# Leaving 110 groups of constant products out of a planned two-layer attention kernel, with a new order for every engine

## The chip, the core and the metric

The kernel runs on one core of a Trainium2 chip. The metric is device time in microseconds (us) of one execution: the lower, the better. TensorE is called PE, VectorE DVE, ScalarE ACT, GpSimd POOL, and SyncE, which issues most of the DMAs, SP. L944 is line 944 of the kernel before.

## The reference, cut to what matters

Four attention layers in a row, A, B, A, B, each added to its input (2048 positions, 512 features, 32 heads of 16):

```
def _A_ref(x, wqkv, wo):          # window of 8 positions, 2 apart
    q, k, v = split(x @ wqkv)
    logits = einsum("bhsd,bhswd->bhsw", q, k[pos - 2*w]) * scale
    o = einsum("bhsw,bhswd->bhsd", softmax(masked logits), v[pos - 2*w])
    return o @ wo
def _B_ref(x, wqkv, wo):          # causal, the last 256 positions
    scores = masked(einsum("bhqd,bhkd->bhqk", q, k) * scale)
    return einsum("bhqk,bhkd->bhqd", softmax(scores), v) @ wo
x = x + _A_ref(_layernorm(x), A_wqkv, A_wo)
x = x + _B_ref(_layernorm(x), B_wqkv, B_wo)
x = x + _A_ref(_layernorm(x), A_wqkv, A_wo)
x = x + _B_ref(_layernorm(x), B_wqkv, B_wo)
```

## The kernel before, in words

The 2048 positions are cut into 8 chunks of 256. For each of the two A, B pairs of layers and each chunk, `layer_a` and then `layer_b` add their work to a plan, so that there are 16 units A0, B0, A1, B1 to A15, B15. Ahead of them `prep` (scopes pA and pB) loads the weights and splits each into two fp16 parts.

Every piece of work is a task on one engine. A layer normalises (`norm`, L875: statistics on DVE at L888, the power at L897 on POOL, the scaled copy `xn` at L915 on ACT, four transposes on PE at L919, the halves `xh` on ACT and `xl` on DVE), projects (`proj_t`, L944 to L946, and `proj_n`, L964 to L967, on PE, three fp16 products for each fp32 one), attends and then projects out (`finish`, L978: `oh` on ACT, `ol` on POOL or DVE, `proj_n`, and the sum `x` on DVE at L995). Layer A attends with products of q and k on DVE or POOL (L1077), sums over the head on PE (L1085), a softmax on DVE and ACT, weights spread on PE (L1154), products with v on DVE (L1167) and sums on POOL (L1174 to L1176) or DVE. Layer B computes the scores twice: once for the row maximum (PE L1262 and L1265, DVE L1284 and L1280, or L1276 in the first chunk of a layer) and once for the exponential (PE L1356 and L1358, ACT L1362, a mask on POOL at L1371), and then the values (PE L1388). The last unit has a tail of its own: `divide` on DVE (L1404 to L1407), moves by DMA (L1413), and the last `finish`.

The order of all this is not left to a scheduler. The table `ORDER` has one list of whole numbers for each scope, one number for each task: tasks of one engine run in the ascending order of these places (`order`, L558). A negative entry -1-p puts the task on its other engine, at place p. So the table settles each engine's queue, SP's with its DMAs among them. `order` walks the queues with costs of its own only to choose PSUM banks and buffers; among its constants is a model of a TensorE clock that falls when recent work was thin (L643 and L644).

Scope W, which the change leaves out, has 110 tasks on PE (L1491 to L1499). Each takes a free PSUM bank and runs three fp16 products of the constant `selt` with itself, 128x128 by 128x256; nobody reads what they write:

```
    plan.begin("W")
    for i in range(IDLE):
        junk = Banks(psum, 1, [P, 512])

        def idle(junk=junk):
            for _ in range(3):
                nc.tensor.matmul(junk.t[:, 0 : 2 * P], selt[:, 0], selt.rearrange("p g k -> p (g k)"), start=True, stop=True)

        plan.add("PE", 0.33, idle, w=[Val(junk)], mode="F", act=0.32)
```

Of their 110 places, 46 are at or below 145 and 24 from 217 to 461 (the beginning of PE's queue, up to the first pair of layers), and 40 are at 3427 or above, out of 3606 (the last unit).

Of the kernel before, what the change touches and what calls it, by code (L numbers as in the profile page):

```python
# [25 lines left out]
W = 8  # L26
# [14 lines left out]
    "pA": [2, -7, 1, 0, 3, 2, 7, 6, 9, 8, 15, 6, 12, 3, 2, 4, 3, 5, 7, 10, 10, 14, 16, 10, 18, 11, 19, 7, 9, 5, -9,  # L41
        14, 9, 17, 21, 21, 19, 34, 15, 28, 10, 13, 8, 12, 34, 41, 39, 53, 45, 54, 25, 52, 24, 75],
    "pB": [12, 14, 11, 18, 52, 59, 51, 71, 53, 33, 98, 30, 61, 15, 20, 13, 21, 76, 85, 60, 91, 62, 91, 38, 92, 37,
        78, 17, 29, 16, 26, 82, 92, 64, 100, 68, 41, 93, 40, 84, 18, 36, 14, 35, 96, 97, 71, 115, 74, 79, 43, 99, 42,
        83, 20, 29, 30, 2, 21, 22, 19, 20],
    "W": [11, 89, 70, 122, 80, 108, 1, 87, 112, 81, 84, 90, 83, 86, 109, 73, 13, 0, 102, 145, 88, 68, 143, 139, 128,
        126, 105, 107, 125, 137, 104, 142, 113, 99, 94, 72, 103, 78, 114, 127, 141, 12, 106, 101, 138, 110, 251, 313,
        217, 280, 273, 268, 238, 275, 274, 276, 270, 260, 248, 264, 278, 259, 237, 241, 318, 277, 267, 323, 461, 437,
        3431, 3432, 3427, 3497, 3464, 3468, 3479, 3441, 3463, 3483, 3490, 3507, 3485, 3484, 3500, 3502, 3493, 3557,
        3574, 3571, 3583, 3589, 3576, 3579, 3581, 3575, 3569, 3578, 3577, 3585, 3586, 3570, 3588, 3582, 3489, 3558,  # L50
        3580, 3587, 3564, 3584],
    "A0": [0, 0, 2, 1, 3, 4, 3, 5, 1, 4, 5, 11, 4, 8, 7, 13, 0, 1, 15, 16, 17, 18, 19, 20, 22, 23, 32, 35, 37, 40,
        45, 46, 47, 49, 16, 22, 24, 25, 26, 27, 28, 29, 30, 31, 33, 36, 38, 39, 43, 44, 48, 50, 17, 23, 54, 55, 56,
        57, 58, 61, 62, 63, 64, 65, 66, 67, 74, 75, 77, 79, 27, 32, 5, 7, 32, 30, 31, 33, 42, 37, 35, 36, 38, 51, 41,
        43, 40, 42, 60, 48, 50, 49, 47, 69, 28, 6, 55, 56, 31, 57, 58, 59, 34, -9, 93, 63, 9, 65, 10, 95, 66, 11, 67,
        -70, 98, 70, 12, 72, 14, 111, 76, 15, 73, -78, 39, 13, 116, 117, 118, 119, 120, 121, 123, 124, 80, 44, -82,
        129, 130, 131, 132, 133, 134, 135, 136, 85],
    "B0": [82, 86, 87, 88, 89, 16, 90, 46, 144, 48, 97, 45, 140, 47, 95, 147, 148, 155, 156, 162, 165, 166, 167, 149,
        152, 153, 154, 157, 158, 160, 161, 54, 103, 53, 102, 24, 26, 28, 27, 25, 23, 38, 36, 43, 45, 150, 163, 170,
        176, 181, 182, 184, 185, 159, 164, 168, 169, 171, 172, 174, 175, 56, 105, 55, 104, 33, 32, 35, 31, 34, 37,  # L60
        40, 39, 41, 42, 242, 245, 247, 249, 250, 254, 255, 256, 65, 243, 246, 258, 261, 263, 266, 269, 271, 68, 244,
        134, 227, 124, 234, 132, 222, 119, 221, 118, 235, 128, 226, 125, 253, 136, 137, 66, 139, 44, 46, 284, 70,
        290, 71, 33, 308, 283, 69, 295, 73, 32, 310, 75, 287, 151, 297, 156, 279, 146, 272, 145, 292, 153, 286, 154,
        281, 149, 282, 148, 159, 74, 161, 47, 48, 321, 81, 322, 82, 35, 396, 371, 91, 377, 93, 36, 413, 102, 317,
        173, 326, 177, 298, 158, 312, 169, 314, 170, 320, 176, 316, 172, 311, 171, 178, 85, 180, 49, 50, 408, 101,
        394, 96, 38, 450, 404, 99, 407, 100, 40, 462, 115, 309, 167, 353, 184, 378, 192, 370, 191, 363, 186, 372,
        190, 354, 185, 364, 187, 193, 94, 194, 69, 71, 433, 106, 427, 103, 41, 442, 438, 109, 444, 110, 43, 451, 112,
        72, 74, 77, 79, 251, 78, 80, 267, 268, 126, 56, 503, 504, 505, 506, 507, 508, 509, 510, 282, 83, 128, 58,
        514, 515, 516, 518, 519, 520, 521, 522, 289, 84],
    "A1": [9, 20, 24, 22, 26, 27, 4, 29, 49, 146, 52, 101, 50, 151, 51, 100, 17, 18, 177, 179, 180, 186, 187, 188,  # L70
        189, 192, 196, 199, 202, 203, 204, 207, 208, 211, 57, 59, 173, 178, 183, 190, 191, 193, 194, 195, 197, 198,
        200, 201, 205, 210, 212, 213, 58, 60, 209, 214, 216, 218, 220, 223, 225, 229, 219, 228, 230, 231, 232, 236,
        239, 240, 61, 63, 21, 23, 109, 106, 108, 107, 206, 112, 111, 113, 110, 215, 115, 117, 116, 114, 224, 120,
        123, 122, 121, 233, 126, 127, 62, 129, 130, 131, 64, 133, 252, 138, 26, 135, 25, 257, 141, 27, 140, -143,
        265, 143, 28, 147, 30, 262, 144, 31, 150, -153, 67, 29, 285, 288, 289, 291, 293, 294, 296, 299, 157, 72,
        -156, 300, 301, 302, 303, 304, 305, 306, 307, 162],
    "B1": [160, 164, 163, 165, 166, 34, 168, 76, 315, 78, 174, 77, 319, 79, 175, 329, 331, 333, 335, 336, 337, 339,
        340, 324, 328, 330, 338, 341, 342, 343, 344, 87, 181, 88, 183, 51, 52, 55, 54, 53, 56, 64, 63, 67, 68, 334,
        346, 347, 348, 349, 351, 356, 357, 327, 345, 350, 358, 359, 361, 362, 365, 89, 188, 90, 189, 61, 57, 59, 60,
        62, 58, 66, 65, 70, 73, 423, 435, 436, 439, 440, 441, 445, 446, 111, 452, 453, 454, 456, 458, 459, 460, 463,  # L80
        114, 443, 229, 230, 415, 216, 218, 416, 215, 217, 412, 209, 210, 403, 203, 204, 426, 220, 222, 432, 223, 227,
        448, 232, 234, 236, 113, 238, 75, 76, 473, 119, 476, 120, 52, 488, 469, 117, 486, 123, 53, 499, 479, 121,
        470, 118, 55, 500, 497, 127, 487, 124, 59, 524, 134, 449, 233, 237, 472, 256, 258, 464, 242, 243, 455, 241,
        245, 482, 259, 260, 468, 250, 252, 465, 244, 248, 471, 253, 255, 264, 125, 273, 81, 82, 536, 138, 523, 133,
        61, 550, 528, 135, 535, 137, 60, 551, 561, 146, 542, 140, 63, 606, 548, 142, 562, 147, 64, 607, 155, 501,
        277, 281, 527, 290, 293, 529, 291, 292, 513, 285, 287, 502, 278, 280, 485, 263, 265, 498, 272, 276, 512, 283,
        286, 294, 136, 295, 86, 87, 598, 154, 579, 151, 67, 619, 621, 160, 608, 156, 68, 636, 618, 159, 638, 164, 72,
        652, 635, 163, 625, 161, 71, 653, 170, 554, 306, 309, 555, 307, 308, 568, 312, 314, 609, 328, 330, 599, 321,
        323, 604, 322, 325, 549, 302, 305, 567, 311, 315, 331, -333, 333, 104, 106, 643, 166, 646, 167, 74, 668, 654,
        171, 657, 172, 77, 678, 658, 173, 669, 175, 80, 684, 676, 177, 673, 178, 81, 687, 181, 108, 105, 113, 114,  # L90
        384, 115, 117, -92, 400, 190, 92, 724, 725, 726, 727, 728, 729, 730, 731, 414, 120, 192, -412, 733, 734, 735,
        739, 740, 741, 742, 743, 417, 121],
    "A2": [6, 44, 46, 23, 25, 94, 19, 96, 80, 325, 83, 179, 84, 332, 86, 182, 22, 24, 352, 355, 360, 366, 367, 368,
        369, 373, 385, 386, 387, 390, 391, 393, 397, 399, 92, 97, 374, 375, 376, 379, 380, 381, 382, 383, 384, 388,
        389, 392, 398, 400, 401, 402, 95, 98, 409, 410, 411, 417, 419, 420, 421, 428, 406, 418, 422, 424, 429, 430,
        431, 434, 104, 107, 37, 42, 196, 195, 198, 197, 395, 200, 201, 202, 199, 405, 207, 208, 206, 205, 414, 211,
        213, 212, 214, 425, 219, 221, 105, 224, 225, 226, 108, 228, 447, 231, 44, 235, 45, 457, 240, 47, 239, 46,
        466, 247, 50, 246, 48, 467, 249, 51, 254, -258, 116, 49, 474, 475, 477, 478, 480, 481, 483, 484, 262, 122,
        -262, 489, 490, 491, 492, 493, 494, 495, 496, 269],
    "B2": [266, 270, 271, 274, 275, 57, 279, 129, 511, 130, 284, 131, 517, 132, 288, 526, 530, 531, 534, 537, 538,  # L100
        540, 541, 525, 532, 539, 543, 544, 545, 546, 547, 139, 300, 141, 303, 93, 89, 88, 91, 90, 95, 100, 102, 107,
        116, 552, 559, 569, 570, 571, 572, 573, 574, 533, 553, 557, 558, 560, 563, 564, 565, 150, 316, 149, 317, 94,
        92, 99, 96, 98, 97, 101, 103, 109, 111, 641, 649, 655, 659, 660, 661, 664, 665, 174, 667, 670, 671, 672, 675,
        677, 681, 683, 180, 663, 361, 363, 634, 345, 346, 639, 349, 350, 626, 340, 342, 620, 338, 339, 651, 354, 357,
# [349 lines left out]
IDLE = 110  # L454
# [1082 lines left out]
```

## Time and profile before

| what | value |
| --- | --- |
| time, median of 3 runs | 1459.28 us (1456.88 to 1462.84) |
| time of the profiled execution | 1460.25 us |
| its span, first to last instruction | 1458.5 us |
| mean granted TensorE clock in it | 0.971 |
| PE busy, DVE busy | 1365.3 us, 1210.2 us |
| HBM read, written | 50.33 MB, 35.09 MB |

Busy times are shares of the span; the profiled execution's 1460.25 us are the span and 1.75 us around it. In a table of windows, each row is a stretch of the span with the busy time of the engines in it, the number of instructions (x), the granted clock (1.00 is full speed, 0.50 half), the share of the DMA engines and their GB/s. Matmuls are pipelined and overlap, so busy PE time says that one was under way, not that the array was full.

### The profile page before, as it was taken

The page shows a single profiled execution, that of the slowest core. Times are in us where ns is not written, and L with a number is a line of the kernel's source. Part 1 is how long each engine was busy: PE and PEld are TensorE (multiplying, and loading weights), DVE is VectorE, ACT ScalarE, POOL GpSimd, SP SyncE. Part 2 cuts the span into 40 slices and gives each one's busy share as a digit, 9 for nine tenths or more (in the row PEclk, how much of TensorE's full clock was granted, in tenths as well). Part 3 has the DMA queues.
Part 4 walks back from the last instruction along what each step waited for, and adds up shares of the span by engine and source line. Part 5 has one row for each costly group of instructions (what it writes and reads, how often), then busy time and mean ns, then how long its engine had stood idle before and what let it go on. Part 6 is the DMA issues. An engine that isn't in the chain of part 4 may idle for free.

```text
span 1458.5 us, 35237 instructions
## 1 busy us (share of the span) xinstructions
PE 1365.3 (94%) x14058; PEld 792.0 (54%) x14058; DVE 1210.2 (83%) x2312; ACT 738.7 (51%) x1050; POOL 660.9 (45%) x754
## 2 busy tenths in 40 slices
PE   7889989999899998999999998998999999999998
PEld 4464645547365463745547363654647456474544
DVE  7959698797978979798897879888797988979694
ACT  6522345454555555555554444555454555545654
POOL 2505054373735627263472615446372642727242
PEclk9899999999999999999999998999999999999999
DMA  7030112222221221312212222222213122122221
GB/s 260 19 89 18 57 44 67 71 51 82 53 82 48 57 81 38 96 29 80 64 51 82 54 88 49 71 63 62 76 48 96 33 76 64 43 90 55 70 69 46
DMA packets 89221, 97.40 MB, mean 67 GB/s; under 512 B 34016, under 2 KB 60128, under 8 KB 89056
## 3 DMA queue, kind: packets, MB, share of 16 engines
q1 hardware_dynamic: 88800, 94.89, 23.3%
q8 instruction: 110, 1.80, 0.5%
q14 instruction: 55, 0.45, 0.1%
q10 hardware_dynamic: 256, 0.26, 0.1%
HBM read 50.33 MB, written 35.09 MB: 59 GB/s over the span
## 4 chain that ended last, share of the span: by engine, by line
PE 56%; DVE 23%; POOL 8%; issue 6%; DMA 3%; ACT 3%; SPq 1%; ACTq 0%; DVEq 0%; POOLq 0%
PE banks L944 9%; PE banks L945 8%; PE banks L946 8%; PE banks L1388 6%; DVE m L1280 5%; PE banks L1085 4%; PE banks L1356 4%; PE banks L966 3%; DVE pw L1167 3%; PE banks L964 3%; DVE banks L1284 3%; PE banks L967 3%; POOL pw L1174 3%; PE banks L1262 3%; PE banks L919 2%
## 5 line engine op out<-in xcount | busy, mean ns | idle before, releaser
L1362 ACT ACTIVATE p<-banks,sclB 128x768 f32<-128x768 f32 x480 | 420.8, 900 | 263.4 <-PE banks L1358 198.0
L1371 POOL TENSOR_SCALAR_AFFINE_SELECT p<-p 128x1024 f32<-128x1024 f32 x240 | 263.8, 1107 | 425.9 <-ACT p L1362 396.1
L1280 DVE TENSOR_REDUCE m<-banks 128x2 f32<-128x512 f32 x448 | 300.4, 686 | 6.1
L1284 DVE COPY_PREDICATED banks<-maskt,banks 128x256 f32<-128x256 int16 x448 | 181.4, 422 | 84.9 <-PE banks L1265 80.2
L1388 PE MATMUL banks<-p,v 128*32 128x128 f32 (+1 forms) x3840 | 196.0, 331 | 7.0 <-POOL p L1371 5.7
L1077 DVE TENSOR_TENSOR pr<-kv,q 128x512 f32<-128x512 f32 x228 | 160.2, 758 | 29.7 <-PE banks L1085 13.3
L1356 PE MATMUL banks<-stk,stk 64*128 64x256 f16 x960 | 138.2, 282 | 28.7 <-DVE m L1280 11.4
L1388 PEld LDWEIGHTS banks<-p,v 128*32 128x32 f32 x3840 | 106.2, 109 | 99.7 <-issue 36.2
L1167 DVE TENSOR_TENSOR pw<-banks,kv 128x1024 f32<-128x1024 f32 x128 | 153.3, 1212 | 2.8 <-PE banks L1154 1.2
L1174 POOL TENSOR_TENSOR pw<-pw 128x512 f32<-128x512 f32 x101 | 129.5, 1283 | 26.9 <-DVE pw L1167 26.8
L1265 PE MATMUL banks<-stk,stk 48*128 48x128 f16 (+1 forms) x1024 | 127.4, 249 | 4.0 <-DVE m L1276 1.6
L1262 PE MATMUL banks<-stk,stk 48*128 48x128 f16 (+1 forms) x896 | 112.5, 252 | 16.9 <-DVE m L1280 6.6
L1356 PEld LDWEIGHTS <-stk 64*128 64x128 f16 x960 | 56.5, 94 | 114.3 <-issue 108.5
L1358 PE MATMUL banks<-stk,stk 64*128 64x128 f16 x960 | 109.7, 221 | 0.0
L1262 PEld LDWEIGHTS <-stk 48*128 48x128 f16 x896 | 50.7, 94 | 104.9 <-issue 98.1
L915 ACT ACTIVATE xn<-x,rs 128x512 f32<-128x512 f32 x64 | 52.1, 814 | 63.8 <-DVE rs L900 54.2
L1175 POOL TENSOR_TENSOR pw<-pw 128x256 f32<-128x256 f32 x101 | 73.9, 732 | 7.9
L1085 PE MATMUL banks<-pr,sel 128*32 128x512 f32 x512 | 70.0, 602 | 0.9 <-DVE pr L1077 0.6
L944 PE MATMUL banks<-xh,wB1h 128*128 128x256 f16 x256 | 70.7, 276 | 0.1
L944 PE MATMUL banks<-xh,wA2h 128*128 128x256 f16 x256 | 70.6, 276 | 0.0
L944 PE MATMUL banks<-xh,wA0h 128*128 128x256 f16 x256 | 70.6, 276 | 0.0
L946 PE MATMUL banks<-xh,wA0l 128*128 128x256 f16 x256 | 70.2, 274 | 0.2 <-DVE wA0l L864 0.2
(184 smaller groups left out, 3070.1 us busy)
## 6 DMA issues: line engine op xcount, KB each, us to landing
stk<-re SPq DMA_DIRECT2D x256, 96.0 KB
re<-eh SPq DMA_DIRECT2D x128, 128.0 KB
re<-el SPq DMA_DIRECT2D x64, 128.0 KB
oc<-os SPq DMA_DIRECT2D x120, 64.0 KB
os<-scr SPq DMA_DIRECT2D x15, 512.0 KB
x<-in_A_x_dram SPq DMA_DIRECT2D x8, 512.0 KB
xd<-x SPq DMA_DIRECT2D x16, 256.0 KB
x<-xd SPq DMA_DIRECT2D x8, 512.0 KB
```

What stands on the lines that cost most here:

```text
L944: nc.tensor.matmul(ps[mp].t[:, i], wh, xh, start=k == 0, stop=False)
L946: nc.tensor.matmul(ps[mp].t[:, i], wl, xh, start=False, stop=k == 3)
L1077: E.tensor_mul(pr.t, window(kv[1].t, m, 64 * tq, 64)[:, 0], qb)
L1167: nc.vector.tensor_mul(pw.t, pb.t.unsqueeze(1).broadcast_to([P, 2, W, 64]), v)
L1174: E.tensor_add(t[:, :, 0:4], t[:, :, 0:4], t[:, :, 4:8])
L1262: nc.tensor.matmul(ps.t[:, par, 0 : (2 - qb) * P], lhs, stk[hf, bef][r, col, qb * P :], start=True, stop=True)
L1280: nc.vector.tensor_reduce(out=m.t[:, :, u, qb], in_=ps.t[:, :, 0 : 2 * P], op=ALU.max, axis=AX.X)
L1284: nc.vector.copy_predicated(t[:, :, 0:P], maskt[:, 0:P].bitcast(I16).unsqueeze(1).broadcast_to([P, 2, P]), t[:, :, 2 * P : 3 * P])
L1356: nc.tensor.matmul(o[:, two], k[:, jf * P : (jf + 1) * P], q, start=True, stop=True)
L1362: nc.scalar.activation(pt.t[:, :, 2 * i : 2 * i + 2].rearrange("p s m q -> p m s q"), ps.t[:, :, : 3 * P].rearrange("p m (s q) -> p m s q" ...
L1371: nc.gpsimd.affine_select(out=v, in_=v, pattern=[[0, 8], [-1 if b == 0 else 1, P]], compare_op=ALU.is_gt if b == 0 else ALU.is_ge, fill=0. ...
L1388: nc.tensor.matmul(o, v[:, jj, 17 * h : 17 * h + 32], rhs, start=z == 0 and (b == 0 or first), stop=z == 1 and b == 1, tile_position=(0, 3 ...
```

## The change: what it does

`IDLE` goes from 110 to 0, so that the loop over scope W adds no task, and the list "W" leaves the table. The other lists are all replaced: each engine's queue is in a new order. No other line changes; the work of the reference is done by the same tasks with the same shapes. By the signs of the entries, 87 tasks are on their other engine: 19 products of L1077 go from DVE to POOL and 19 from POOL to DVE; of the multiplications at L1462, 7 go from DVE to POOL and 4 back; of the differences at L989, 7 go from DVE to POOL and 3 back; at L1128, 1 and 2; and of the small scalings at L1304 and L1306, 15 go from ACT to DVE and 10 back. Compared by their sequence, PE's queue is the old one with neighbours exchanged, no task more than 27 places from its old one; in SP's queue none is more than 12 places away, in DVE's 50, in POOL's 31, in ACT's 19.

```
 ORDER = {
...
-    "W": [11, 89, 70, 122, 80, 108, 1, 87, 112, 81, 84, 90, 83, 86, 109, 73, 13, 0, 102, 145, 88, 68, 143, 139, 128,
-        126, 105, 107, 125, 137, 104, 142, 113, 99, 94, 72, 103, 78, 114, 127, 141, 12, 106, 101, 138, 110, 251, 313,
-        217, 280, 273, 268, 238, 275, 274, 276, 270, 260, 248, 264, 278, 259, 237, 241, 318, 277, 267, 323, 461, 437,
-        3431, 3432, 3427, 3497, 3464, 3468, 3479, 3441, 3463, 3483, 3490, 3507, 3485, 3484, 3500, 3502, 3493, 3557,
-        3574, 3571, 3583, 3589, 3576, 3579, 3581, 3575, 3569, 3578, 3577, 3585, 3586, 3570, 3588, 3582, 3489, 3558,
-        3580, 3587, 3564, 3584],
...
-IDLE = 110
+IDLE = 0
```

811 rows, old and new, of the table ORDER are left out of this document.

## The prediction

> **What bounds the kernel now.** I read the page first: busy shares, the slices with the granted clock, and the chain that ended last.
>
> ```profile
> span 1458.5 us, 35237 instructions
> ...
> PE 1365.3 (94%) x14058; PEld 792.0 (54%) x14058; DVE 1210.2 (83%) x2312; ACT 738.7 (51%) x1050; POOL 660.9 (45%) x754
> ...
> PEclk9899999999999999999999998999999999999999
> ...
> PE 56%; DVE 23%; POOL 8%; issue 6%; DMA 3%; ACT 3%; SPq 1%; ACTq 0%; DVEq 0%; POOLq 0%
> ```
>
> The kernel is bound by PE with DVE close behind it, and PE's clock isn't always full. Next I asked for the removed line, L1497, by windows: two stretches near the beginning, one near the end, and the whole.
>
> ```profile
> 69.70:82.50 12.80, 2.78 (x21) 0.87 0.22 33
> 120.00:135.50 15.50, 6.06 (x44) 1.00 0.06 14
> 1402.10:1419.10 17.00, 4.97 (x33) 1.00 0.24 53
> ...
> 0.00:1458.50 1458.50, 48.35 (x330) 0.97 0.24 67
> ```
>
> The 330 products keep PE busy for 48.35 us. That is no saving of 48 us: they stand where PE would otherwise wait. The question is what they do for the clock. PE's windows around two falls of the clock:
>
> ```profile
> 47.00:50.40 3.40, 1.36 (x8) 1.00 0.01 2
> 50.40:57.20 6.80, 6.80 (x30) 0.50 0.00 1
> 306.40:309.80 3.40, 2.06 (x29) 1.00 0.44 99
> 309.80:313.20 3.40, 3.40 (x25) 0.50 0.65 157
> ```
>
> After 3.4 us in which PE was busy for 1.36 (40%) or for 2.06 (61%), the clock is 0.50 for 3.4 us or twice that. The timeline shows what it costs, in half and in full clock, for fp16 products of one shape:
>
> ```profile
> 71.97 0.63 PE L967 MATMUL banks<-wA3l,oh 128*128 128x512 f16 x1
> 72.40 0.63 PE L964 MATMUL banks<-wA3h,ol 128*128 128x512 f16 x1
> ```
>
> ```profile
> 1450.05 0.38 PE L966 MATMUL banks<-wB3h,oh 128*128 128x512 f16 x1
> 1450.26 0.38 PE L967 MATMUL banks<-wB3l,oh 128*128 128x512 f16 x1
> ```
>
> From one start to the next it is 0.43 us at 0.50 and 0.21 us at 1.00. So a granted stretch of 3.4 us at half clock loses up to 1.7 us where PE sets the time.
>
> **The change, part by part.** The sum is made against the profiled execution's own 1460.25 us (span 1458.5 and 1.75 around it), which is 0.97 us above the median of 1459.28.
>
> (1) The products' own time on the path. They issue no DMA and nobody reads them; what waits is the PE work queued behind them. The chain, in order of time, has these longest pieces of L1497:
>
> ```profile
> 79.49 0.98 PE banks L1497 x9
> ...
> 155.06 0.75 PE banks L1497 x3
> ...
> 1395.93 0.70 PE banks L1497 x6
> ...
> 1434.63 0.66 PE banks L1497 x6
> ```
>
> Together 3.09 us at most, and nothing at least. The first stands between two groups of transposes, the second of which needs ACT's next `xn`; so I count it as covered and take the other three: 0.75 + 0.70 + 0.66 = **-2.1 us** (bounds -3.1 and 0).
>
> (2) The beginning. All instructions by windows:
>
> ```profile
> 69.70:82.50 12.80, 8.08 (x42) 4.23 (x42) 10.45 (x20) 4.01 (x6) 1.76 (x5) 0.87 0.22 33
> 82.50:107.00 24.50, 24.46 (x222) 20.44 (x222) 11.46 (x17) 6.65 (x11) 0.52 (x2) 1.00 0.38 104
> 120.00:135.50 15.50, 13.15 (x87) 6.35 (x85) 14.30 (x33) 2.56 (x5) 10.84 (x13) 1.00 0.06 14
> 160.00:1340.00 1180.00, 1122.98 (x11819) 649.31 (x11817) 999.87 (x1847) 603.71 (x858) 564.91 (x625) 0.97 0.23 64
> 1402.10:1419.10 17.00, 14.56 (x194) 8.00 (x191) 16.31 (x32) 11.10 (x16) 7.77 (x7) 1.00 0.24 53
> ```
>
> From 69.7 to 82.5 PE has 8.08 - 2.78 = 5.30 us of its own work, 41% of the stretch, like the 40% ahead of the first fall. So it should come to 82.5 at half clock, and from there to 107 PE is busy 24.46 of 24.5 us: what it loses there isn't hidden. One stretch of half clock costs 1.7 us. The transposes ahead of it are on the path too:
>
> ```profile
> 78.83 0.66 PE L919 MATMUL banks<-idf,xn 128*128 128x128 f32 x4 [2.83 <-ACT xn L915]
> ```
>
> At half clock I estimate 0.4 us more for such a group, the 0.66 without the part that doesn't follow the clock, for two groups 0.8. I take **+2.5 us**; the bounds are 0 (the clock recovers before 82.5, or the new order brings other work there) and 2 x 1.7 + 0.8 = 4.2. From 120 to 135.5, 13.15 - 6.06 = 7.09 us (46%) are left, so the clock should fall earlier there too; but DVE is busy for 14.30 of 15.5 us and POOL for 10.84, and I cost it at nothing. If that cover were gone, it would be one more stretch, 1.7 us.
>
> (3) The last unit's scores, 1402.1 to 1419.1. PE keeps 14.56 - 4.97 = 9.59 us of 17 (56%), less than the 61% ahead of the second fall. At half clock 9.59 becomes 19.18 us, 2.2 more than the stretch, and DVE (16.31 of 17 us) has no slack to wait for a late score. Bounds: 0 (the clock holds) and 8.5 (everything stretched, 17 us at half speed). I take the 2.2 and one stretch of 1.7, since half clock is granted in whole stretches: **+3.9 us**.
>
> (4) The end. The last `finish` waits for a DMA, and PE's timeline has this:
>
> ```profile
> 1442.76 5.45 PE L1497 MATMUL banks<-selt 128*128 128x256 f16 x48
> 1449.04 0.39 PE L966 MATMUL banks<-wB3h,oh 128*128 128x512 f16 x1 [0.83 <-ACT oh L987]
> ```
>
> Without these 48 products PE is empty for 6 us before the last 24 products, which end the kernel with DVE's sum behind them and run at 0.21 us each. They would begin at half clock. Windows of the clock that follow the 3.4 us grid of the rows above (1446.4, 1449.8, 1453.2) put 1449.0 to 1453.2 at half, a loss of 4.2 / 2 = **+2.1 us**. Bounds: 0, and 24 x 0.22 = 5.2 if the whole stage were at half clock.
>
> (5) The rest of the order. Between 160 and 1340 there is next to nothing of scope W. The 87 tasks that change engine leave POOL 6 more tasks on balance (+3 at L1462, +4 at L989, -1 at L1128). The dearest kind:
>
> ```profile
> L1462 POOL TENSOR_TENSOR oc<-oc,os x10: 1264/1276/1784, 313.6 to 1414.8; 128x512 f32<-128x512 f32 x10
> ```
>
> Six of those are 8 us of the 798 in which POOL is idle: nothing, and 1.28 us for each if one were waited for. All the exchanged neighbours, in SP's queue of DMAs too, can matter through PE's gaps: in the 1180 us PE is idle for 57, and a mean clock of 0.97 means some 35 us lost, 92 in all, or 7 us for each of the 13 units that fit there (1180 / 1458.5 x 16). Nothing in the profile says whether the new queues leave more or fewer such gaps. I take **0**, and bounds of two units, -14 and +14.
>
> Sum: -2.1 + 2.5 + 3.9 + 2.1 + 0 = +6.4, so 1466.65 for the profiled execution and **1465.7** against the median, 0.4% slower.
>
> A page's rule weighed against this. The Trainium skill (TensorE: Matmul & The Clock Gate, "What's actually happening") puts the fall to half clock after an idle window of about 3.4 us. By that, (2) and (3) would cost nothing, and only (4), where PE is empty, would be lost. The rows above differ: 29 matmuls and 2.06 us of work ran in the window ahead of the second fall.
>
> **The rivals.** (a) **Only emptiness lowers the clock, not thin work.** For it: where the products now fill an empty PE, as in (4), they plainly act. Against it: the window from 306.4. Then (2) and (3) are 0, and -2.1 + 2.1 = 0: 1459.3, not slower; that is the rule just cited. (b) **The new order closes gaps in the middle.** With two units' worth less, 1465.7 - 14 = 1451.7, on the other side. For it: queues made without the products have PE free for real work in the same places. Against it: there are none of them in the middle, and PE is already busy for 1122.98 of 1180 us there. It decides from one unit (7 us) on. (c) **The new order opens gaps in the middle**: a unit and a third more, 9 us, gives 1475. For and against it stands the same row; PE has 57 us of idle time there, DVE 180, and a task one place too late opens a gap and pays for the clock too. That the change does nothing at all can't be: 330 products are gone.
>
> **How the numbers follow.** Forecast 0.50, (a) 0.17, (b) 0.12, (c) 0.21. A measurement of this kernel can tell about 0.5%, 7.3 us, from no change: faster is below 1452.0, slower above 1466.6. The forecast's own range is 1460 to 1471, and its middle lies close to the border: I give 0.27 of its 0.50 to the same and 0.23 to slower. With (a) and 0.03 of (b) that makes 0.47 for the same, 0.09 for faster, and 0.23 + 0.21 = 0.44 for slower. The range takes in (a), most of (b) and half of (c), and the bounds of terms 1 to 4 except where all are at their worst: 1451 to 1477.
>
> **What would show it.** Step 1: no L1497, and the queue behind it earlier by a few tenths at these places. Step 2: a granted clock of 0.50 around 80, and a later end of the stretch that PE fills (107 now). Step 3: half clock between 1395 and 1420, where it is 1.00 now. Step 4: the last products at 0.43 us from start to start, at least the first of them. Step 5: PE's idle time and mean clock between the same units. The prediction is wrong if the clock stays at 1.00 in steps 2 and 3, or if the middle moves by more than all the rest.

## The result, and the profile after

| | kernel before | changed kernel |
| --- | --- | --- |
| median of 7 runs | 1462.2 us (1456.88 to 1465.21) | 1471.43 us (1466.42 to 1474.11) |
| ratio | 1 | 1.0063, 95% interval 1.0049 to 1.0077 |
| profiled execution | 1460.25 us | 1471.43 us |

The change costs 0.63%, some 9 us; the forecast was 6.4 us. The page of the changed kernel, beside that of before:

```profile
span 1469.7 us, 34604 instructions
...
PE 1340.8 (91%) x13728; PEld 767.2 (52%) x13728; DVE 1207.1 (82%) x2311; ACT 737.3 (50%) x1045; POOL 671.0 (46%) x760
...
PEclk9688898999999999999999998999999999999988
```

PE has 24.5 us less to do, and the span is 11.2 us longer. The clock line differs in slices 2 to 5 and 7 of the 40 and in the last two. (Line numbers of the changed kernel are 7 lower: L988 is the sum `x`, L995 of before.) Its PE by windows, in the beginning:

```profile
46.70:77.40 30.70, 16.26 (x48) 0.50 0.02 3
77.40:80.80 3.40, 0.23 (x1) 1.00 0.10 15
80.80:91.10 10.30, 7.30 (x32) 0.50 0.34 48
91.10:114.00 22.90, 22.86 (x207) 1.00 0.39 112
```

PE comes to the stretch that it fills (82.5 to 107 before) at half clock, as step 2 said, and for three granted stretches of 3.4 us where I had counted one: in these 10.3 us PE was busy for 7.30 only. All engines, in the middle and around the last unit's scores:

```profile
160.00:1340.00 1180.00, 1123.23 (x11789) 649.42 (x11789) 995.15 (x1852) 604.75 (x858) 566.51 (x625) 0.97 0.23 64
...
1412.00:1415.40 3.40, 2.29 (x36) 1.39 (x31) 3.37 (x9) 3.40 (x6) 0.31 (x1) 1.00 0.04 8
1415.40:1422.20 6.80, 6.34 (x68) 3.19 (x67) 5.86 (x14) 3.15 (x5) 2.92 (x3) 0.50 0.44 81
```

The middle has PE busy for 1123.23 of 1180 us (1122.98 before) at the same 0.97. In the scores the clock falls after a stretch with PE busy for 2.29 of 3.4 us. And the end, in the timeline:

```profile
1457.36 0.61 PE L959 MATMUL banks<-wB3h,oh 128*128 128x512 f16 x1 [6.23 <-ACT oh L980]
1457.76 0.63 PE L960 MATMUL banks<-wB3l,oh 128*128 128x512 f16 x1
...
1463.28 0.38 PE L959 MATMUL banks<-wB3h,oh 128*128 128x512 f16 x1
1463.49 0.38 PE L960 MATMUL banks<-wB3l,oh 128*128 128x512 f16 x1
```

PE is empty for 6.23 us, then runs at about 0.42 us from start to start until 1463.28, and only then at 0.21.

To see where the time goes, I follow two points through all kernels: the start of DVE's second sum `x` of A1, and the end of the last sum. In before and after, the first of them is

```profile
146.49 0.75 DVE L995 SCALAR_TENSOR_TENSOR x<-banks,sclA,x 128x512 f32<-128x512 f32 x1
```

```profile
153.76 0.75 DVE L988 SCALAR_TENSOR_TENSOR x<-banks,sclA,x 128x512 f32<-128x512 f32 x1
```

7.27 us are lost by then, and at the end 10.85 (1466.38 against 1455.53). At the 44th of the 64 sums, which ends at 1015.7 us in before, the difference is 8.7 us, and at the 60th (1360.7) it is 7.7. In between single sums go from +5.2 (the 34th, 840.5) to +12.1 (the 9th, 311.5). So two thirds of the loss are there after the first 150 us, little is added on balance up to the last unit, and 3.2 us come in the last unit.

### The profile page after: what moved, and what is told of

Read it like the earlier page. It is cut to its first block, busy times and chain, and to the rows that moved or that the text cites. A ratio compares the mean times of both kernels' runs of the same rounds, so it can differ in the third digit from the quotient of the medians.

```text
span 1469.7 us, 34604 instructions
## 1 busy us (share of the span) xinstructions
PE 1340.8 (91%) x13728; PEld 767.2 (52%) x13728; DVE 1207.1 (82%) x2311; ACT 737.3 (50%) x1045; POOL 671.0 (46%) x760
## 4 chain that ended last, share of the span: by engine, by line
PE 55%; DVE 23%; POOL 7%; issue 6%; DMA 4%; ACT 3%; SPq 2%; ACTq 0%; DVEq 0%; POOLq 0%
PE banks L937 10%; PE banks L938 9%; PE banks L939 9%; PE banks L1381 5%; DVE m L1273 5%; PE banks L1078 4%; DVE banks L1277 4%; PE banks L1349 3%; PE banks L959 3%; DVE pw L1160 3%; PE banks L957 3%; PE banks L960 3%; PE banks L1255 2%; POOL pw L1167 2%; PE banks L912 2%
## 5 line engine op out<-in xcount | busy, mean ns | idle before, releaser
L1381 PE MATMUL banks<-p,v 128*32 128x128 f32 (+1 forms) x3840 | 199.6, 334 | 6.2 <-POOL p L1364 4.7
L1258 PE MATMUL banks<-stk,stk 48*128 48x128 f16 (+1 forms) x1024 | 128.8, 250 | 5.2 <-DVE m L1269 2.1
L1255 PE MATMUL banks<-stk,stk 48*128 48x256 f16 (+1 forms) x896 | 112.8, 253 | 22.3 <-DVE m L1273 11.0
L908 ACT ACTIVATE xn<-x,rs 128x512 f32<-128x512 f32 x64 | 52.0, 812 | 70.7 <-DVE rs L893 61.4
L938 PE MATMUL banks<-xl,wA0h 128*128 128x256 f16 x256 | 70.7, 276 | 0.4 <-DVE xl L918 0.4
L938 PE MATMUL banks<-xl,wB1h 128*128 128x256 f16 x256 | 70.9, 277 | 0.0
```

The costliest lines, as they stand in the source:

```text
L938: nc.tensor.matmul(ps[mp].t[:, i], wh, xl, start=False, stop=False)
L1255: nc.tensor.matmul(ps.t[:, par, 0 : (2 - qb) * P], lhs, stk[hf, bef][r, col, qb * P :], start=True, stop=True)
L1381: nc.tensor.matmul(o, v[:, jj, 17 * h : 17 * h + 32], rhs, start=z == 0 and (b == 0 or first), stop=z == 1 and b == 1, tile_position=(0, 3 ...
```

## The experiments

My theory: the products hold the clock, and without them it is half in the beginning and in the last unit (clock theory). The rivals: the new queues cost the time (order), and only an empty PE lowers the clock (emptiness). "A1" and "end" in the table are the two points above, in us against the profile of before. A ratio here is not the quotient of two medians, and the medians of the same runs give other differences from before: 7.8 us for e1 (5.3 by its ratio), 5.9 for e3 (5.3), 2.2 for e4 (0), 12.5 for e2 (10.8), 9.2 for the changed kernel (9.2). So a difference of less than some 2.5 us can't be told from one ratio. The line numbers of these kernels differ, since their tables `ORDER` differ in length.

| kernel | ratio (95% interval) | A1 | end |
| --- | --- | --- | --- |
| changed kernel | 1.0063 (1.0049 to 1.0077) | +7.27 | +10.85 |
| e1, old order, no products | 1.0036 (1.0024 to 1.0048) | +3.80 | +7.90 |
| e3, old order, first 70 groups | 1.0036 (1.0021 to 1.0050) | -0.17 | +8.22 |
| e4, old order, last 40 | 1.0000 (0.9989 to 1.0011) | +2.57 | +3.96 |
| e9, old order, all but 16 | 1.0007 (0.9992 to 1.0023) | -0.62 | +1.10 |
| e7, old order, narrow products | 0.9999 (0.9983 to 1.0016) | -1.42 | +2.28 |
| e8, old order, 35 more | 1.0065 (1.0045 to 1.0084) | +0.30 | +9.04 |
| e2, new order, 110 put back | 1.0074 (1.0047 to 1.0101) | +7.70 | +15.75 |
| e6, new order, last 40 put back | 1.0055 (1.0035 to 1.0074) | +6.15 | +11.39 |
| e5, new order, 17 PE tasks in the old sequence | 1.0064 (1.0042 to 1.0087) | +8.52 | +14.37 |
| e11, old beginning, new rest | 1.0056 (1.0039 to 1.0074) | +2.78 | +8.07 |
| e12, new beginning, old rest | 1.0067 (1.0043 to 1.0091) | +7.89 | +12.22 |
| e13, old first 72 us, new rest | 1.0057 (1.0035 to 1.0078) | +5.47 | +6.32 |

A warning for reading it: one profile is one execution. e3 and before have the same queues and products up to the last unit, and at the 44th sum e3 is 2.9 us later. So the differences in the last column carry some 3 us that belong to no edit; those at A1 carry some 0.6 us (e3, e8 and e9 have the same queues as before up to there).

**e1: the products alone.**

```
-IDLE = 110
+IDLE = 0
```

> The old queues, with the 110 groups of products left out and nothing else changed. Clock theory (the products hold the clock, and the order matters little): 7 to 11 us above the kernel before, half clock from about 47 to 77 as in the changed kernel, unit 1 (the sum x of A1 and B0) ends 6 to 8 us later, the middle is unchanged. Rival, order (the 9 us come from the new queues): within 3 us of the kernel before, or faster by up to the 3 us that the products take on the chain. Rival, emptiness (only an empty PE lowers the clock): half clock is added at the very end alone, 0 to 3 us above before.

Measured: 1.0036, some 5 us (7.8 by the medians). The order rival falls in its pure form, and so does emptiness, since the clock falls on thin work too. The clock theory's own 7 to 11 us is missed by the ratio, and its 6 to 8 us at A1 is missed by the profile. Windows of PE in e1, with the clock in the column after the count:

```profile
1411.00:1414.40 3.40, 1.91 (x32) 1.00 0.32 49
1414.50:1424.80 10.30, 9.12 (x96) 0.50 0.31 68
```

32 matmuls and 1.91 us of work stand ahead of three stretches of half clock. By the ratios e1 isn't as slow as the changed kernel, but only just: the intervals end at 1.0048 and begin at 1.0049, and by the medians the two are 1.4 us apart. The profile says more. e1's sum of A1:

```profile
150.29 0.75 DVE L989 SCALAR_TENSOR_TENSOR x<-banks,sclA,x 128x512 f32<-128x512 f32 x1
```

It is 3.80 us late, about half of the 7.27. So by the profile the new queues cost something of their own.

**e2: the new order with the products put back**, each group ahead of the PE task that it preceded before.

```
+    "W": [0, 0, 8.1, 8.3667, 8.6333, 62.1, 65.1, ... 3479.8, 3479.85],
-IDLE = 0
+IDLE = 110
```

> The new queues, with the 110 groups of products put back ahead of the same PE tasks as before. Clock theory: within 3 us of the kernel before, half clock in the first 100 us for about 10 us and not 41. Rival, order: 7 to 11 us above the kernel before although the clock is held.

Measured: 1.0074. The clock theory had it within 3 us of before; it is 10.8 us above by the ratio, 12.5 by the medians (1474.45 and 1461.92). The clock is held, and that doesn't help:

```profile
core 0: 1474.6 us, clock 0.972
```

That is before's 0.971. It is not clean evidence for the order, though: in the new queues the products also stand in the way. In e2's timeline, ahead of A1's last projection, there is

```profile
138.37 4.02 PE L1491 MATMUL banks<-selt 128*128 128x256 f16 x18
```

4.02 us of products at half clock, with scores behind them for which DVE waits 3.56 us (until 142.76).

**e3 and e4: one end each.** `IDLE = 70` with the places below 1000, and `IDLE = 40` with those above.

> The old queues with only the 70 groups of the beginning. Clock theory: 1.5 to 4 us above the kernel before, all of it after 1340 us, most of it in the last 24 products at half clock (the prediction's steps 3 and 4, 6 us, would be the upper end). Rival, order or middle: 0. If the thin scores of the last unit lose the 3.9 us that the prediction gave them, this kernel is 4 to 6 us above before.

> The old queues with only the 40 groups of the last unit. Clock theory: 5 to 8 us above the kernel before, all of it in the first 150 us; the two kernels that keep one end each add up to the one that keeps neither. The prediction's step 2 alone would give 2.5 us.

Measured: e3 1.0036, so by the times the 40 groups of the last unit carry the 5 us; e4 1.0000, where the clock theory had 5 to 8 us. As it expected, the two add up to e1. In e3's profile the loss at A1 is gone and the last unit is late: +3.01 us at the sum that ends at 1360.7 in before, +6.45 at that of 1435.4, +8.22 at the end. That is 3.4 for the scores and 1.8 for the end. e1, the same old order without products, has less in its profile: +5.77, +6.63 and +7.90 at these points, so 0.9 and 1.3. With the 40 in place the last unit loses 0.2 us in e4 and -0.5 in e7. So the profiles put the 40 groups between 2.1 and 5.2 us. e4's profile has 2.57 us at A1, of which its ratio shows nothing (bounds -1.6 and +1.6) and its medians 2.2: what the first 70 groups are worth lies between 0 and 2.6 us, and I can't say closer.

**e9: the 16 groups of the empty stretch alone** left out, of the 110.

```
(the places 3574 to 3589 leave "W")
-IDLE = 110
+IDLE = 94
```

> The kernel before without the 16 groups that run while PE waits for the last DMA (1442.8 to 1448 us); the other 94 stay. Prediction's step 4: 1.4 to 2.1 us above before (1.001), the first of the last 24 products 0.43 us from start to start. Rival (the products of the last unit are worth their 5 us through this empty stretch alone): 1.003 or more.

Measured: 1.0007, and +1.10 us at the end (-0.32 at 1435.4, so 1.4 after it). The last products in its timeline:

```profile
1448.71 0.61 PE L961 MATMUL banks<-wB3h,oh 128*128 128x512 f16 x1 [6.21 <-ACT oh L982]
...
1452.44 0.38 PE L961 MATMUL banks<-wB3h,oh 128*128 128x512 f16 x1
```

Half clock from 1448.71 to 1452.3, 3.6 us at a loss of 1.8 (step 4 had 4.2 and 2.1). So by difference the other 24 groups, not those of the empty stretch, carry most of e3's 5 us; the intervals of e9 (up to 1.0023) and e3 (from 1.0021) just overlap.

**e7: narrow products**, 32 columns of the array instead of 128.

```
-nc.tensor.matmul(junk.t[:, 0 : 2 * P], selt[:, 0], ...
+nc.tensor.matmul(junk.t[0:32, 0 : 2 * P], selt[:, 0, 0:32], ...
```

> The kernel before with the same 330 products, each 32 columns of the array wide instead of 128: PE is as busy, a quarter of the array works. If the clock follows how much of the array works: like the old queues without products, half clock for 140 to 150 us in all, 4 to 8 us above before. Rival, it follows busy time: half clock for 80 to 95 us in all, within 2 us of before.

Measured: 0.9999. The rival holds: for the time it doesn't matter that a quarter of the array works. Half clock adds up to 99 us by the trace, a little more than the rival had, and 85 in before; but up to 166 us, where most of the products stand, it is 17 us (24 in before), and after 1350 there is none in either. PE by windows in e7, where before had half clock:

```profile
47.00:50.40 3.40, 2.04 (x14) 1.00 0.01 2
50.40:57.20 6.80, 6.49 (x53) 1.00 0.00 1
```

**e8: products in the middle's gaps.** 35 groups more, ahead of tasks that PE waits for: `IDLE = 145`, with 35 fractional places added to W.

> The kernel before with 35 more groups of products, put into the gaps of 0.4 to 1.7 us that PE has ahead of nine of the ten falls of the clock between 160 and 1340 us. If the clock is what those gaps cost: six or more of the ten falls go and the time is 5 to 15 us below before. Rival, the gaps cost by the wait itself and the clock's part lies beside DVE's work: within 3 us of before; or the products come into the path of what waits, up to 8 us above it.

Measured: 1.0065, slower. All engines of e8 in the middle:

```profile
160.00:1340.00 1180.00, 1126.39 (x11889) 655.52 (x11891) 993.33 (x1837) 600.14 (x855) 560.18 (x620) 0.98 0.24 64
```

The mean clock is 0.98 (0.97 before), so a little of it is held: 47.8 us of half clock in this stretch against 61.4. But there are still ten falls, since three went where six or more were expected and three came in other places, and time is lost all the same. One place shows why, four groups ahead of A4's spread (L1149 of e8, L1154 of before). Before:

```profile
384.12 0.39 PE L1154 MATMUL banks<-eh,selt 32*128 32x512 f16 x2 [1.43 <-DVE m L1280]
```

and e8:

```profile
385.03 2.48 PE L1492 MATMUL banks<-selt 128*128 128x256 f16 x12 [1.43 <-DVE m L1275]
387.45 0.61 PE L1149 MATMUL banks<-eh,selt 32*128 32x512 f16 x2
```

The gap is 1.43 us in both, and both end with DVE's `m`. By the code each group takes a PSUM bank, like the spread behind it. They didn't run in the gap but waited through it, and then put 2.48 us ahead of real work. Around this place e8's difference goes from +0.9 (325.5 in before) to +3.8 (398.8). It isn't so everywhere: of the 35 groups, 20 stand in blocks that began after a wait of 0.4 to 1.4 us like this one, and 15 in blocks that began without one.

**e5: where the new order loses.** In the changed kernel's timeline PE waits 4.59 us for ACT's `v`, with scores and A1's last projection behind:

```profile
139.25 0.40 PE L1349 MATMUL banks<-stk,stk 64*128 64x256 f16 x2 [4.59 <-ACT v L1222]
```

```
 (PE's places 214 to 230, the same 17 tasks, 16 of them at another place)
-B0.133 B0.114 B0.120 B0.139 B0.131 B0.141 B0.122 B0.127 ... A1.124 A1.125 ...
+B0.133 B0.131 B0.139 B0.141 B0.120 B0.114 A1.124 B0.137 B0.127 A1.125 ...
```

> The changed kernel with 17 neighbouring PE tasks around 134 to 150 us (A1's last projection, B0's scores) in the old sequence; nothing else differs. Order theory (in the changed kernel A1's last projection stands behind 12 score tasks, one of which waits 4.6 us): 1.5 to 3.5 us below the changed kernel, about 1469 us, and the sums x of A1 end 1.5 to 3.5 us earlier in the profile (+3.8 to +5.8 against before, where the changed kernel has +7.3). Rival, clock alone: within 1 us of the changed kernel, since half clock from 139 to 149 slows the stretch in any sequence.

Measured: 1.0064, and A1 no earlier. My theory of that place falls. In e5's timeline the wait is still there, at another task:

```profile
139.17 0.29 PE L887 MATMUL banks<-stk,stk 48*128 48x128 f16 x2 [4.61 <-ACT v L851]
```

What PE waits for sits in ACT's queue, here in the changed kernel's timeline:

```profile
138.08 0.62 ACT L980 CAST oh<-o 128x512 f16<-128x512 f32 x1 [7.40 <-POOL o L1169]
138.61 0.59 ACT L1222 ACTIVATE v<-banks 128x512 f32<-128x512 f32 x1
```

`v` stands behind A1's `oh`, which waits for POOL's sums. PE's sequence doesn't decide it. Nor is ACT's sequence new at this place, since e1, with the old queues, has the same pair:

```profile
135.91 0.62 ACT L981 CAST oh<-o 128x512 f16<-128x512 f32 x1 [6.46 <-POOL o L1170]
136.44 0.59 ACT L1223 ACTIVATE v<-banks 128x512 f32<-128x512 f32 x1
```

There PE waits 2.04 us for `v`. The changed kernel comes to this place later: POOL's first sum of A1 begins at 130.25 us in it and at 128.11 in e1 (123.54 in before). Which tasks of the new queues lose these 2.1 us and the rest up to the sums, no run shows.

**e6: the last 40 in the new order.** W put back with the 40 places of the last unit.

> The new queues with only the 40 groups of the last unit put back. If the products of the last unit are worth the same in both orders (5 us in the old one, where leaving them out cost 0.36%): 3 to 5.5 us below the changed kernel, 1.002 to 1.004 of before. Rival, the new queues were made for a clock that falls there: 0 to 2 us below the changed kernel, 1.005 or more of before.

Measured: 1.0055 against the changed kernel's 1.0063: at most a small part of the 5 us comes back, and the intervals overlap. The rival's number fits better, its reason isn't shown: e6's trace has no half clock from 1340 to 1468, and yet its scores are 3.8 us later (+9.40 at the sum of 1360.7, +13.24 at 1435.4), of which 1.9 come back at the end (+11.38). As in e2, the products may stand in the way there; I didn't follow it.

**e11, e12, e13: which part of the order.** `ORDER` put together from both, with no products; all engines change over at the same tasks.

> No products. All engines run the tasks up to the end of A1's sums in the old order (some 165 us), and the rest in the new one. If the new order's own loss lies in the beginning: 1.003 to 1.0045 of before, like the old queues without products, with the sums of A1 3 to 4.5 us late; rival, it lies in the rest: 1.0055 or more.

> No products. The reverse: the new order up to the end of A1's sums, the old one for the rest. If the new order's own loss lies in the beginning: 1.0055 to 1.007 of before, with the sums of A1 6.5 to 8 us late; rival: 1.003 to 1.004.

> No products. Only the first 72 us (weights and A0) in the old order, the rest new. If the beginning's loss has two parts, 1.5 us in the weights and A0 and 2 us in A1 and B0: the sums of A0 about 1 us late and those of A1 5 to 6 us, 1.0045 to 1.0055 of before. Rival, all of it in the first part: A1 3 to 4.5 us late; all in the second: 6.5 us or more.

Measured: 1.0056, 1.0067 and 1.0057, too close for the times to tell apart; by its time e11 even goes with its rival. The profiles do tell them apart at A1. The sum in e11 and in e12:

```profile
149.27 0.74 DVE L618 SCALAR_TENSOR_TENSOR x<-banks,sclA,x 128x512 f32<-128x512 f32 x1
```

```profile
154.38 0.74 DVE L618 SCALAR_TENSOR_TENSOR x<-banks,sclA,x 128x512 f32<-128x512 f32 x1
```

All five kernels with the whole new beginning (the changed one, e2, e5, e6, e12) have +6.15 to +8.52 at A1, whatever products they have; the three with the old beginning and no products there (e1, e4, e11) have +2.57 to +3.80. So the new beginning costs about 4 us by A1, and e13 (+5.47) puts some 2 of them into the first 72 us. But e11, without that loss, is at +7.05 at the sum that ends at 316.2 in before: the rest of the new order loses 4 us there. The joint, where the two orders meet, isn't the reason, since the changed kernel, which has none, goes from +7.3 at A1 to +12.1 and +10.3 at the sums that end at 311.5 and 316.2, while e1 and e12, with the old rest, stay there within 1.1 us of their difference at A1. Later the new order takes 2 to 4 us of this back: at the sum that ends at 1360.7 e11 is at +4.8 and the changed kernel at +7.7.

## Why the prediction was right, and where it was not

**The forecast's direction held, and its range by the ratio**: 0.63% slower, with 0.44 given to slower by over 0.5% and 0.47 to the same. The median of 1471.43 us is just above the range's 1471, but before was slower in these seven runs too (1462.2, where the forecast started from 1459.28); the ratio puts 1459.28 at 1468.5. The interval's lower end, 1.0049, is at the border of 0.5%.

**Step 1**, -2.1 us, was not measured by itself.

**Step 2** (+2.5) has the right mechanism and is about 1 us too small. Half clock was there, for three stretches instead of one (the counts in the last section say how busy PE has to be before it ends), and a group of transposes took longer as estimated, 1.12 us against 0.66:

```profile
81.45 1.12 PE L912 MATMUL banks<-idf,xn 128*128 128x128 f32 x4 [3.82 <-ACT xn L908]
```

What the stretch lost can be read between the second sum of A0 (it ends at 75.80 in before; +2.61 in the changed kernel, +0.87 in e1) and DVE's first products of A1. In before and after these are

```profile
99.98 2.50 DVE L1077 TENSOR_TENSOR pr<-kv,q 128x512 f32<-128x512 f32 x4 [2.42 <-ACT kv L1058]
```

```profile
105.96 2.50 DVE L1070 TENSOR_TENSOR pr<-kv,q 128x512 f32<-128x512 f32 x4 [1.28 <-ACT kv L1051]
```

That is +5.98, and +4.55 in e1 (104.53): 3.4 us in the changed kernel and 3.7 in the old order. The stretch from 120 to 135.5, set to nothing, adds nothing in the old order, where the loss at A1 is 2.6 to 3.8 us by the profiles. By e4's ratio the whole beginning is worth about nothing there.

**Steps 3 and 4** (+3.9 and +2.1, less the pieces of step 1) have the right mechanism, and their 4.6 us in all is the upper part of what was measured: 3.4 and 1.8 in e3, but 0.9 and 1.3 in e1, 1.4 to 1.8 for the end alone in e9. In the changed kernel the last unit loses 1.9 and 1.3, 3.2 us in all.

**Step 5** (0) is the one that failed. I set the new order to nothing in the middle, where the changed kernel's difference indeed goes only from 7.9 us (at 228.9 in before) to 9.2 (at 1348.8), and never priced it in the beginning, though the diff shows the queues of pA to B0 replaced like all others. There it costs about 4 us (e12 and the changed kernel against e1, e4 and e11). The middle isn't flat either, it loses some 4 us by 311.5 and takes them back. That the sum came out near is in part luck: the beginning lost 7.3 instead of 2.5 less step 1, the last unit less than forecast.

**Rival (a)**, only emptiness, is out (e1's window above). The rule of the Trainium skill that stood beside it (TensorE: Matmul & The Clock Gate, "What's actually happening": half clock after an idle window of about 3.4 us) is too narrow for this kernel by these rows: PE was busy for 1.91 of 3.4 us in e1, and 2.29 in the changed kernel, ahead of a fall. **Rival (c)**, order, is half true, in a place that it didn't name. **Rival (b)** didn't happen.

**Still open**: which tasks of the new queues lose the 4 us of the beginning, and why the two losses don't add. The products alone cost 0.36%, the new order with the products 0.74%, and both changes together 0.63%. e2 shows one reason, products that stand in the way of the new queues; how much of the 0.74% that is wasn't measured.

## What to carry to other kernels

Work that only keeps a clock up is worth what the next real work on that engine gains: here 2 to 5 us in the last unit, whose scores are thin, and 0 to 2.6 us in the beginning. Such filler should not need what the waiting work needs: in e8, groups that by the code take a PSUM bank waited through the gap, and then stood in front. And a queue searched anew is a change of its own: run the old order without the edit before putting a difference down to the edit.

## What the runs showed of the hardware

Products a quarter as wide hold the clock as well as full ones for the time (e7, 0.9999).

The clock is not a matter of emptiness alone. In the traces it changes at multiples of 3.4 us, so I cut all fourteen (of the kernel before and the thirteen of the table above) into these stretches and set the busy share of PE in each against the clock of the next. After a stretch at full clock:

| PE busy in the stretch | stretches | followed by half clock |
| --- | --- | --- |
| under 40% | 53 | 53 |
| 40 to 60% | 134 | 107 |
| 60 to 70% | 154 | 70 |
| 70 to 85% | 428 | 18 |
| over 85% | 4662 | 0 |

After a stretch at half clock the way back is harder: with PE busy under 80% none of 152 was followed by full clock, with 80 to 95% 15 of 101, over 95% 226 of 239. So in this kernel thin work both lowers the clock and keeps it low; the shares are of profiled busy time, which holds the overlap of matmuls.

A higher mean clock is no gain by itself: e2's profile has 0.972 and its runs a median of 1474.45 us, the changed kernel, with the same queues and no products, 0.951 and 1471.43 us.
